# First layer's loop: rows sent ahead of the lists on GpSimd, the token copy moved up, the noise indices' copy moved down, the gate's last remainder moved up

## The chip, the cores and the metric

The kernel runs on one core of one Trainium2 chip. The metric is the device time of one execution in microseconds. All times below are microseconds unless marked ns.

## What is computed

The reference is three stages, one after another, in float32:

- **Attention without a softmax over the keys.** q is softmaxed over its 64 head dimensions, k over its 576 positions; per batch and head (8 by 8) the output is q_s @ (k_sᵀ @ v). The result is 4608 tokens of 512 numbers.
- **Layer one, a mixture of 8 experts with one choice.** `logits = x @ w_gate`, the expert with the largest logit gets the token: `h = relu(x @ w1[e])` with 1024 columns, `y = h @ w2[e]`, times the softmax weight of that expert.
- **Layer two, a mixture of 8 experts with two choices and noise.** `noisy = x @ w_gate + log1p(exp(x @ w_noise)) * noise`; the two largest experts of each token are computed and added with their softmax weights.

## The kernel before

The attention writes one row per token to a table in HBM (`xg`). Tokens are sorted into lists by expert (`lists`, one row of four words per token and choice: token, weight, row of the noise, padding). Both expert layers then go through the lists in blocks of 128 tokens. Every float32 matmul with the weights is done as three fp32r products: high part of x times high part of W, low part of x times high part of W, high part of x times low part of W. So a block costs 96 matmuls of 128x128 by 512 columns: 12 each for the two halves of the first product (`b.m0`, `b.m1`, in PSUM as `pk` and `pkv`), 24 for the second (`b.y0`, `b.y1`, in `pq`); the hidden layer of one block and the output of the block before it run in one turn of the loop, so one turn has 48 of them.

**The loop in question** is `step1` (line 569), the body of `moe1`'s loop over the blocks of layer one; it runs 38 times. Each engine runs its own instructions in the order in which `step1` writes them, and semaphores hold it where it needs another's result. One turn does, beside the 48 matmuls:

- **The gate of layer two** for the 128 tokens that the turn before produced (`x2r`, written by ScalarE in `b.result()`, line 545). TensorE transposes them (`gate_pe1`), ScalarE and VectorE split them into three bf16 parts: `part16` is ScalarE's cast, `rest16` (line 309) VectorE's remainder. `gate_parts` makes the first part and the first remainder, `gate_parts2` the second part and the last remainder (both take the same two lines, 304 and 309). `gate_products` (line 326) has TensorE multiply the three parts with the gate's weights: 12 small matmuls, the last four of which read the last remainder. The sum, three activations and two chains of small VectorE operations (`gate_chain1`, `gate_chain2`) give each token's two experts; `gate_rank` (line 388) has TensorE rank the tokens of each expert, from `g_os` (line 374), and `gate_places` (line 403) gives each token its places in the lists (`g_di`).
- **GpSimd's four kinds of transfer.** `send_list` adds to a table (`dump`, line 408) and writes the 128 tokens with two indirect transfers into the lists of layer two (line 411). `send_rows` (line 421) writes the tokens' 128 rows back to `xg`, at the token numbers in `tk`. `gather` (line 271) fetches the 128 rows of a later block from `xg` into `xr`; it waits until the rows sent before it have landed. `gather_noise` (line 277) fetches the noise of the next block into `nz`, at the indices in `ni`.
- **The copies `gate_meta`**: `gate_row` (line 346, marks padding), `ni` (line 562) and `tk` (line 563), all from `meta`, which holds the list rows of four blocks in flight: iB is the block whose output is made, iA the one behind it. `next_meta` (lines 439 and 440) shifts all four on by one.
- **Weights.** Each turn prepares a part of the next expert's weights in two halves: a 512 KB load into `raws[0]` or `raws[1]` (line 151, on SyncE's queue), a high half cast by ScalarE (`prep_hi`, lines 157 to 159) and a low half by VectorE (`prep_lo`, lines 164 and 165, the second of which is the copy called `tick`).
- **SyncE's queue**, in this order: zeros for 128 rows of the output (line 549), two weight loads (line 151), the next list row block into `iN` (`load_list`, line 266, which waits until the lists sent have landed), and four transfers of the hidden layer (`spread`, line 530).
- **The hidden layer's turn**: ScalarE's relu (`relu32`, line 521), VectorE's transpose in blocks of 32 (`turn32`, line 525), `spread` to `hT`, then the high and low parts (`hi32`, line 536, `lo32`, line 541) in the next turn.

The tile framework puts the waits: an instruction that overwrites a tile waits until the transfers that read it are done. So `ni` (line 562) waits for the noise gather of the turn before, and the copy into `tl` (line 369, in `gate_chain2`) waits for the two list transfers of its turn.

Of the kernel before, what the change touches and what calls it, by code (L numbers as in the profile page):

```python
# [73 lines left out]
def reg(eng, expr, lo, hi):  # L74

    return eng.snap(eng.to_reg(expr), min_val=lo, max_val=hi)
# [71 lines left out]
def load_part(nc, z, raw, i, c0=0, n=SL):  # L148

    a = z.wall[i] if isinstance(i, int) else z.wall[ds(i, 1)].rearrange("o p x -> (o p) x")  # L150
    return nc.sync.dma_start(raw, a[:, c0:c0 + n])


def prep_hi(nc, z, off, h):

    raw = z.raws[h]
    nc.scalar.activation(z.touch[h], raw[:, 0:1], AF.Identity, bias=z.tick[h], scale=1.0)
    no_mm(z, nc.scalar.copy(cols(z, off + h * HL, HL), raw), h)  # L158
    nc.scalar.copy(z.touch[h], raw[:, 0:1])  # L159


def prep_lo(nc, z, off, h):
    raw = z.raws[h]
    no_mm(z, nc.vector.tensor_sub(cols(z, off + 8192 + h * HL, HL), raw, f32(cols(z, off + h * HL, HL))), h)  # L164
    nc.vector.tensor_copy(z.tick[h], raw[:, 0:1])
# [89 lines left out]
def transposes(nc, z, out, src):  # L255
    for c in range(4):
        nc.tensor.transpose(out[:, c * 128:(c + 1) * 128], src[:, c * 128:(c + 1) * 128], z.ident)  # L257


def col(z, x, c):  # L260
    return z.meta[:, c, z.cols[id(x)]:z.cols[id(x)] + 1] if id(x) in z.cols else x[:, c:c + 1]


def load_list(nc, z, to, row):

    nc.sync.dma_start(to, z.lists[row:row + 128, :] if isinstance(row, int) else z.lists[ds(row, 128), :])


def gather(nc, z, of, n=None):

    return nc.gpsimd.indirect_dma_start(  # L271
        out=z.xr, out_offset=None, in_=z.xg[0:n, :] if n else z.xg,
        in_offset=bass.IndirectOffsetOnAxis(ap=col(z, of, 2 if n else 0), axis=0))


def gather_noise(nc, z, of):
    nc.gpsimd.indirect_dma_start(
        out=z.nz, out_offset=None, in_=z.noise,
        in_offset=bass.IndirectOffsetOnAxis(ap=of, axis=0))
# [22 lines left out]
def part16(z, i, x):  # L302

    return z.tc.nc.scalar.copy(z.x3[i], x)


def rest16(z, i, x):
    out = z.x2T if i == 0 else z.x3[2]
    return z.tc.nc.vector.tensor_tensor(out, x, z.x3[i], op=OP.subtract)
# [13 lines left out]
def gate_products(nc, z):  # L323
    for i in range(3):
        for c in range(4):
            nc.tensor.matmul(z.pL[:, 0:48], lhsT=z.x3[i][:, c * 128:(c + 1) * 128],
                             rhs=z.w3[:, c].rearrange("p i n -> p (i n)"),
                             start=i == 0 and c == 0, stop=i == 2 and c == 3)


def gate_sum(nc, z):
    nc.vector.tensor_reduce(z.gt["lg"], z.pL[:, 0:48].rearrange("p (i n) -> p n i", i=3), axis=AX.X, op=OP.add)


def gate_act(nc, z):
    a, t = nc.scalar, z.gt

    a.activation(t["ab"], t["lg"][:, 8:16], AF.Abs)
    a.activation(t["e"], t["ab"], AF.Exp, scale=-1.0)
    a.activation(t["ln"], t["e"], AF.Ln, bias=z.ones[:, 0:1], scale=1.0)  # L340


def gate_row(nc, z):

    v, t = nc.vector, z.gt
    v.tensor_scalar(t["nv"], col(z, z.iB, 0), float(N), None, op0=OP.is_ge)


def gate_chain1(nc, z):
    v, t = nc.vector, z.gt  # L350

    v.tensor_scalar(t["u"], t["e"], 1.0, None, op0=OP.add)  # L352
    v.scalar_tensor_tensor(t["c"], t["u"], 1.0, t["e"], op0=OP.subtract, op1=OP.subtract)
    v.reciprocal(t["r"], t["u"])
    v.scalar_tensor_tensor(t["ns"], t["lg"][:, 8:16], 0.0, t["ln"], op0=OP.max, op1=OP.add)
    v.tensor_mul(t["c"], t["c"], t["r"])
    v.tensor_sub(t["ns"], t["ns"], t["c"])
    v.tensor_mul(t["ns"], t["ns"], z.nz)
    v.tensor_add(t["ny"], t["ns"], t["lg"][:, 0:8])
# [26 lines left out]
def gate_rank(nc, z):  # L386
    for i, x in enumerate((z.after, z.ones16)):
        nc.tensor.matmul(z.pL[:, 48 + i * E:48 + (i + 1) * E], lhsT=x, rhs=z.gt["os"], start=True, stop=True)


def gate_ends(nc, z):
    v = nc.vector
    v.tensor_tensor(z.gt["rg"], z.pL[:, 48:48 + E], z.ends2, op=OP.add)
    v.tensor_tensor(z.ends2, z.pL[:, 48 + E:48 + 2 * E], z.ends2, op=OP.add)
# [11 lines left out]
def send_list(nc, z):  # L406
    t = z.gt
    nc.gpsimd.tensor_tensor(z.dump, z.dump, z.c256, op=OP.add)
    for k in range(2):
        nc.gpsimd.tensor_tensor(z.spacer, t["di"], t["di"], op=OP.add)  # L410
        i = nc.gpsimd.indirect_dma_start(  # L411
            out=z.lists, out_offset=bass.IndirectOffsetOnAxis(ap=t["di"][:, k:k + 1], axis=0),
            in_=z.tl[:, k, :], in_offset=None)
        z.tc.add_to_no_dep_group("list2", i.ins)
        z.tc.declare_no_dep(i.ins, group="list2", across_iterations=True,
                            reason="each token and choice has its own row")


def send_rows(nc, z, of=None):

    i = nc.gpsimd.indirect_dma_start(
        out=z.xg, out_offset=bass.IndirectOffsetOnAxis(ap=col(z, z.iB, 0) if of is None else of, axis=0),
        in_=z.x2r[:, 0:512], in_offset=None)
    z.sent = i
    for o in z.before_rows:
        z.tc.declare_no_dep(i.ins, o.ins, reason="it reads the rows of tokens that are in no block before it")
    z.tc.add_to_no_dep_group("xg2", i.ins)
    z.tc.declare_no_dep(i.ins, group="xg2", across_iterations=True, reason="each token has its own row")
# [8 lines left out]
def next_meta(nc, z, n=3):  # L437

    nc.vector.tensor_copy(f32(z.meta[:, :, 0:n]), f32(z.meta[:, :, 1:n + 1]))
    nc.vector.tensor_copy(f32(z.meta[:, :, n]), f32(z.iN))  # L440


def turn_x(nc, z):
    transposes(nc, z, z.pX, z.xr)


def make_xhi(nc, z):
    nc.scalar.copy(flat(z.xhi), z.pX)
# [7 lines left out]
def make_xlo(nc, z):  # L456
    nc.vector.tensor_sub(flat(z.xlo), z.pX, f32(flat(z.xhi)))
# [17 lines left out]
def tab_value(eng, tab, row, g, max_val):  # L475
    return eng.value_load(tab[0:1, ds(g + row * 128, 1)], min_val=0, max_val=max_val)
# [71 lines left out]
def zero_rows(nc, z, zr):  # L548
    nc.sync.dma_start(z.out[zr:zr + 128, :] if isinstance(zr, int) else z.out[ds(zr, 128), :], z.yo)


def gate_parts(nc, z):

    gate_pe1(nc, z)
    part16(z, 0, z.pS)
    rest16(z, 0, z.pS)


def gate_meta(nc, z):

    gate_row(nc, z)
    nc.vector.tensor_copy(z.ni, col(z, z.iA, 2))
    nc.vector.tensor_copy(z.tk, col(z, z.iB, 0))


def gate_parts2(nc, z):
    part16(z, 1, z.x2T)
    rest16(z, 1, z.x2T)


def step1(tc, z, g, tab, wm, wy, then):


    nc = tc.nc
    a, v, sp = nc.scalar, nc.vector, nc.sync

    part0 = tab_value(sp, tab, 1, g, 2 * E * K - 1)
    part = tab_value(sp, tab, 1, g + 1, 2 * E * K - 1)
    row = tab_value(sp, tab, 2, g + 3, 2 * E * CAP - 128)
    oa = tab_value(a, tab, 0, g, SLOT + (K - 1) * SL)  # L580
    ov = tab_value(v, tab, 0, g, SLOT + (K - 1) * SL)
    b = Block(z, (wm, wy), True)
    zero_rows(nc, z, reg(sp, smin(g + 2, NT - 1) * 128, 0, N - 128))
    load_part(nc, z, z.raws[0], part0, 0, HL)
    send_list(nc, z)
    b.m0.go(4)
    gate_parts(nc, z)
    prep_hi(nc, z, oa, 1)
    prep_lo(nc, z, ov, 1)
    load_part(nc, z, z.raws[1], part, HL, HL)  # L590
    gate_meta(nc, z)
    send_rows(nc, z, z.tk)
    next_meta(nc, z)
    load_list(nc, z, z.iN, row)
    b.m0.go(8)
    then()
    b.relu32(0)
    b.turn32(0)
    gate_parts2(nc, z)
    for i in range(2):  # L600
        b.hi32(i)
        b.lo32(i)
    b.m1.go(12)
    b.relu32(1)
    b.turn32(1)
    turn_x(nc, z)
    gate_products(nc, z)
    make_xhi(nc, z)
    gather(nc, z, z.iP)
    gate_sum(nc, z)  # L610
    gate_act(nc, z)
    prep_hi(nc, z, oa, 0)
    b.spread()
    make_xlo(nc, z)
    gate_chain1(nc, z)
    gather_noise(nc, z, z.ni)
    gate_chain2(nc, z, z.tk)
    b.y0.go(12)
    b.y1.go(10)
    gate_rank(nc, z)  # L620
    b.y1.go(2)
    gate_ends(nc, z)
    gate_weights(nc, z)
    gate_places(nc, z)
    prep_lo(nc, z, ov, 0)
    b.result()
# [1197 lines left out]
```

## Time and profile before

| | |
|---|---|
| median of 3 runs | 1591.85 us (1590.35 to 1595.33) |
| the profiled execution's own time | 1599.28 us |
| its span in the profile | 1596.7 us |
| TensorE busy | 1515.0 us, 95% of the span |
| VectorE, ScalarE, GpSimd busy | 70%, 54%, 36% |
| mean granted TensorE clock | 0.988 of full speed |

A busy share is an average over the attention (to about 185 us), layer one's loop (to about 716 us), a passage between, and layer two. An engine's idle time counts only where it holds up what sets the end. In the views below, the note in square brackets behind a row is the engine's idle time just ahead of it and what ended it.

### The profile page before, as it was taken

The page shows a single profiled execution, that of the slowest core. Times are in us where ns is not written, and L with a number is a line of the kernel's source. Part 1 is how long each engine was busy: PE and PEld are TensorE (multiplying, and loading weights), DVE is VectorE, ACT ScalarE, POOL GpSimd, SP SyncE. Part 2 cuts the span into 40 slices and gives each one's busy share as a digit, 9 for nine tenths or more (in the row PEclk, how much of TensorE's full clock was granted, in tenths as well). Part 3 has the DMA queues.
Part 4 walks back from the last instruction along what each step waited for, and adds up shares of the span by engine and source line. Part 5 has one row for each costly group of instructions (what it writes and reads, how often), then busy time and mean ns, then how long its engine had stood idle before and what let it go on. Part 6 is the DMA issues. An engine that isn't in the chain of part 4 may idle for free.

```text
span 1596.7 us, 44299 instructions
## 1 busy us (share of the span) xinstructions
PE 1515.0 (95%) x7996; PEld 1216.0 (76%) x7996; DVE 1122.4 (70%) x3052; ACT 867.1 (54%) x1914; POOL 571.4 (36%) x625
## 2 busy tenths in 40 slices
PE   8997899999998999978999999999999999999997
PEld 6876677777776777756788888888887878878885
DVE  6888688877887878875666666666666666666665
ACT  7775355555555555544455555545555555555554
POOL 4576455455444455434222222222222212222221
PEclk9999999999999999999999999999999999999998
DMA  9897666665566556652777787777878777778877
GB/s 323 271 300 207 182 179 177 178 178 143 174 178 174 162 178 156 178 161 59 199 211 213 214 215 218 206 210 210 218 212 206 218 204 212 217 202 219 214 211 184
DMA packets 217312, 318.29 MB, mean 199 GB/s; under 512 B 45312, under 2 KB 143104, under 8 KB 217280
## 3 DMA queue, kind: packets, MB, share of 16 engines
q1 hardware_dynamic: 188624, 255.87, 52.7%
q0 software_dynamic: 28656, 62.03, 18.9%
q8 instruction: 15, 0.25, 0.1%
q14 instruction: 17, 0.14, 0.0%
HBM read 186.85 MB, written 52.31 MB: 150 GB/s over the span
## 4 chain that ended last, share of the span: by engine, by line
PE 51%; DMA 1%; DVE 1%; issue 1%; ACT 0%; SPq 0%; POOLq 0%; ACTq 0%; DVEq 0%
PE pq L243 25%; PE pk L243 13%; PE pkv L243 13%; DMA hT<-h 0%; DMA out<-yo,meta 0%; DMA li<-lists 0%; SPq L530 0%; DMA xr<-xg,li 0%; POOLq L1820 0%; DVE g_u L352 0%; DVE h L525 0%; DVE hlo L513 0%; ACT hhi L536 0%; DVE W L164 0%; PE px L257 0%
## 5 line engine op out<-in xcount | busy, mean ns | idle before, releaser
L243 PE MATMUL pq<-W,hhi 128*128 (+1 forms) x1856 | 495.6, 397 | 6.3 <-ACT W L208 5.0
L243 PEld LDWEIGHTS pq<-W,hhi 128*128 128x128 f32 x1856 | 344.6, 189 | 77.9 <-ACT W L208 5.4
L271 POOL DMA_INDIRECT xr<-xg,meta x114 | 114.7, 1006 | 660.6 <-DVE h L525 436.3
L164 DVE TENSOR_TENSOR W<-raw,W 128x1024 f32 x226 | 277.3, 1227 | 58.5 <-ACT touch L159 39.8
L243 PE MATMUL pk<-W,xhi 128*128 (+1 forms) x936 | 261.8, 401 | 6.3 <-ACT x L1001 2.0
L243 PE MATMUL pkv<-W,xhi 128*128 (+1 forms) x936 | 257.7, 397 | 0.0
L536 ACT CAST hhi<-hT 128x512 fp32r<-128x512 f32 x224 | 127.9, 620 | 233.0 <-PE pkv L243 116.9
L243 PE MATMUL pq<-W,hlo 128*128 (+1 forms) x928 | 252.8, 394 | 0.0
L158 ACT CAST W<-raw 128x1024 f32 x226 | 234.1, 1036 | 0.0
L243 PEld LDWEIGHTS pk<-W,xhi 128*128 128x128 f32 x936 | 174.4, 189 | 59.4 <-issue 19.9
L243 PEld LDWEIGHTS pkv<-W,xhi 128*128 128x128 f32 x936 | 176.9, 189 | 42.9 <-issue 0.4
L243 PEld LDWEIGHTS pq<-W,hlo 128*128 128x128 f32 x928 | 174.3, 189 | 40.1 <-DVE hlo L541 3.0
L541 DVE TENSOR_TENSOR hlo<-hT,hhi 128x512 fp32r<-128x512 f32 x224 | 144.6, 687 | 75.9 <-ACT hhi L536 75.9
L432 POOL DMA_INDIRECT out<-yo,meta x76 | 120.5, 1585 | 179.0 <-issue 176.4
L525 DVE STREAM_TRANSPOSE h<-h 128x512 f32<-128x512 f32 x226 | 160.1, 708 | 9.4 <-ACT h L521 5.3
L462 DVE STREAM_TRANSPOSE raw<-xr 128x512 f32<-128x512 f32 x74 | 81.7, 1104 | 115.7 <-DMA hT<-h 58.6
L243 PE MATMUL pk<-W,xlo 128*128 (+1 forms) x468 | 132.5, 405 | 0.0
L243 PE MATMUL pkv<-W,xlo 128*128 (+1 forms) x468 | 130.2, 399 | 0.0
L471 ACT CAST xhi<-raw 128x512 fp32r<-128x512 f32 x74 | 46.0, 622 | 146.0 <-DMA raw<-raw 118.2
L411 POOL DMA_INDIRECT lists<-tl,g_di x80 | 99.6, 1245 | 16.6 <-issue 13.4
L243 PEld LDWEIGHTS pkv<-W,xlo 128*128 128x128 f32 x468 | 88.0, 188 | 21.4
L243 PEld LDWEIGHTS pk<-W,xlo 128*128 128x128 f32 x468 | 85.8, 190 | 18.5 <-issue 0.2
(315 smaller groups left out, 1823.5 us busy)
## 6 DMA issues: line engine op xcount, KB each, us to landing
raw<-in_wall SPq DMA_DIRECT2D x237, 512.0 KB
hT<-h SPq DMA_DIRECT2D x452, 128.0 KB
raw<-raw SPq DMA_DIRECT2D x296, 64.0 KB
out<-yo SPq DMA_DIRECT2D x41, 256.0 KB
A<-in_q SPq DMA_DIRECT2D x36, 256.0 KB
xg<-xrow SPq DMA_DIRECT2D x36, 256.0 KB
A<-in_v SPq DMA_DIRECT2D x8, 1024.0 KB
A<-in_kT SPq DMA_DIRECT2D x6, 1152.0 KB
```

The source lines that it names most:

```text
L158: no_mm(z, nc.scalar.copy(cols(z, off + h * HL, HL), raw), h)
L164: no_mm(z, nc.vector.tensor_sub(cols(z, off + 8192 + h * HL, HL), raw, f32(cols(z, off + h * HL, HL))), h)
L243: i = z.tc.nc.tensor.matmul(self.out, lhsT=a, rhs=cols(z, self.wo + c, 512), start=self.start and self.n == 0, stop=self.stop and self.n = ...
L271: return nc.gpsimd.indirect_dma_start(out=z.xr, out_offset=None, in_=z.xg[0:n, :] if n else z.xg, in_offset=bass.IndirectOffsetOnAxis(ap=c ...
L411: i = nc.gpsimd.indirect_dma_start(out=z.lists, out_offset=bass.IndirectOffsetOnAxis(ap=t["di"][:, k:k + 1], axis=0), in_=z.tl[:, k, :], i ...
L432: nc.gpsimd.indirect_dma_start(out=z.out, out_offset=bass.IndirectOffsetOnAxis(ap=col(z, z.iB, 0), axis=0), in_=z.yo, in_offset=None, comp ...
L462: nc.vector.transpose(out=z.x32.rearrange("p (c k t) -> p c k t", c=4, k=4), in_=z.xr.rearrange("p (k j c) -> p c k j", k=4, c=4))
L471: nc.scalar.copy(hi, x)
L525: self.nc.vector.transpose(out=to, in_=self.z.h[:, i * 512:(i + 1) * 512].rearrange("p (c x) -> p c x", c=4))
L536: self.nc.scalar.copy(self.z.hhi[i].rearrange("p k (q t) -> p k q t", q=4), self.part32(i))
L541: self.nc.vector.tensor_sub(x, self.part32(i), f32(y))
```

## The change

In `step1`, `gate_meta` and `send_rows` go from behind the second weight load to the front, ahead of `send_list`. `gate_meta` loses the copy into `ni`; it is done late in the turn, after the second `turn32`, from iB, since `next_meta` has by then moved iA's rows there. `gate_parts2` goes from behind the first `turn32` to where `gate_meta` was, directly behind `prep_hi` and `prep_lo` of the second half. Nothing is added or dropped: each turn has the same instructions.

```diff
@@ gate_meta
     gate_row(nc, z)
-    nc.vector.tensor_copy(z.ni, col(z, z.iA, 2))
     nc.vector.tensor_copy(z.tk, col(z, z.iB, 0))
@@ step1
     load_part(nc, z, z.raws[0], part0, 0, HL)
+    gate_meta(nc, z)
+    send_rows(nc, z, z.tk)
     send_list(nc, z)
     b.m0.go(4)
     gate_parts(nc, z)
     prep_hi(nc, z, oa, 1)
     prep_lo(nc, z, ov, 1)
     load_part(nc, z, z.raws[1], part, HL, HL)
-    gate_meta(nc, z)
-    send_rows(nc, z, z.tk)
+    gate_parts2(nc, z)
     next_meta(nc, z)
     load_list(nc, z, z.iN, row)
     b.m0.go(8)
     then()
     b.relu32(0)
     b.turn32(0)
-    gate_parts2(nc, z)
     for i in range(2):
         b.hi32(i)
         b.lo32(i)
     b.m1.go(12)
     b.relu32(1)
     b.turn32(1)
+    nc.vector.tensor_copy(z.ni, col(z, z.iB, 2))
     turn_x(nc, z)
     gate_products(nc, z)
```

## Rows read from the trace of the kernel before

**Rows 1.** Stretches: length, busy PE, PEld, DVE, ACT, POOL; granted clock, transfers' share, GB/s.
```profile
190.00:716.00 526.00, 493.06 (x2644) 385.95 (x2642) 422.09 (x1671) 296.88 (x719) 258.50 (x302) 0.99 0.60 171
...
512.50:518.00 5.50, 5.41 (x19) 4.38 (x20) 4.77 (x23) 2.23 (x8) 1.93 (x2) 0.64 0.46 103
...
452.40:465.80 13.40, 12.96 (x71) 10.20 (x70) 11.07 (x45) 7.84 (x19) 6.59 (x8) 1.00 0.63 143
```

**Rows 2.** Line 421, the rows sent: duration, first and last start, time to landing.
```profile
L421 POOL DMA_INDIRECT xg<-x,tk x38: 960/960/1118, 193.9 to 703.1; - x38
...
DMA to landing us min/median/max: 2.7/5.2/7.5
```

**Rows 3.** Groups by line, 190 to 716 us: busy, mean ns, idle before and releasers.
```profile
L326 PE MATMUL px<-w,x 128*128 128x48 bf16 x456 | 24.2, 184 | 22.7 <-issue 10.1 <-DVE x L309 9.7 <-DVE h L525 3.0
...
L369 DVE COPY tl<-tk 128x2 int32<-128x2 int32 x38 | 5.9, 155 | 1.7 <-DMA lists<-tl,g_di 1.7
...
L562 DVE COPY ni<-meta 128x1 int32<-128x1 int32 x38 | 5.5, 145 | 8.9 <-DMA nz<-in_noise,ni 8.9
```

**Rows 4.** Timeline of TensorE in one turn: start, duration, line, operation, idle before.
```profile
453.57 0.27 PE L326 MATMUL px<-w,x 128*128 128x48 bf16 x4 [0.32 <-issue]
```

**Rows 5.** Timeline of VectorE in the same turn.
```profile
448.52 0.15 DVE L165 COPY tick<-raw 128x1 f32<-128x1 f32 x1
...
450.04 1.24 DVE L164 TENSOR_TENSOR W<-raw,W 128x1024 f32 x1 [0.60 <-ACT touch L159]
...
451.27 0.14 DVE L346 TENSOR_SCALAR g_nv<-meta 128x1 f32<-128x1 int32 x1
...
451.65 0.17 DVE L439 COPY meta<-meta 128x12 f32<-128x12 f32 x1
...
452.87 0.65 DVE L309 TENSOR_TENSOR x<-x,x 128x512 bf16<-128x512 f32 x1
...
457.84 0.15 DVE L369 COPY tl<-tk 128x2 int32<-128x2 int32 x1
...
458.37 0.17 DVE L374 TENSOR_TENSOR g_os<-g_oh 128x8 bf16<-128x8 f32 x1
```

**Rows 6.** Timeline of ScalarE in the same turn: the second part's cast.
```profile
450.33 0.61 ACT L304 CAST x<-x 128x512 bf16<-128x512 f32 x1
```

**Rows 7.** Timeline of GpSimd in this turn and the two behind it.
```profile
447.61 1.05 POOL L408 TENSOR_TENSOR dump<-dump,c 128x2 f32<-128x2 f32 x1 [0.76 <-DVE g_di L403]
...
450.35 1.80 POOL L411 DMA_INDIRECT lists<-tl,g_di  x1 [0.16 <-issue]
452.45 0.96 POOL L421 DMA_INDIRECT xg<-x,tk  x1 [0.30 <-DVE meta L440]
459.50 0.97 POOL L271 DMA_INDIRECT xr<-xg,meta  x1 [6.09 <-DVE ends L394]
...
464.86 1.00 POOL L411 DMA_INDIRECT lists<-tl,g_di  x1 [0.15 <-issue]
...
477.31 2.05 POOL L411 DMA_INDIRECT lists<-tl,g_di  x1 [0.16 <-issue]
```

**Rows 8.** Timeline of SyncE's queue, from this turn into the next but one.
```profile
458.22 2.51 SPq L530 DMA_DIRECT2D hT<-h  x4
...
464.69 1.44 SPq L151 DMA_DIRECT2D raw<-in_wall  x2
471.88 0.33 SPq L266 DMA_DIRECT2D iN<-lists  x1
472.70 2.53 SPq L530 DMA_DIRECT2D hT<-h  x4
...
480.31 1.04 SPq L151 DMA_DIRECT2D raw<-in_wall  x2
481.68 0.33 SPq L266 DMA_DIRECT2D iN<-lists  x1
```

**Rows 9.** Waits of SyncE's queue in the loop: total, times, longest.
```profile
SPq L266 <- DMA lists<-tl,g_di: 94.9, 21, 7.1
```

## Prediction

> **What bounds the kernel now.** I read the page first, for TensorE's high share, then busy time by stretch, then the loop's groups by line, and last the timelines of one turn, engine by engine. By stretch, layer one's loop has TensorE busy for only 493.06 of 526.00 us, 33 us short [rows 1]. All that the change touches lies in that loop. Its 38 turns send their rows first at 193.9 and last at 703.1 us [rows 2], so the mean turn takes 509.2/37 = 13.76 us. One common turn, of 13.40 us, holds 12.96 us of TensorE work [rows 1]. So 12.96 is about the least that a turn can take with these matmuls, and 37 x (13.76 - 12.96) = 30 us is the most that a reordering here can bring.
>
> Where are they? The groups by line give most of TensorE's idle time in the loop to one line: 22.7 us stand ahead of the gate's small products (line 326) [rows 3]. The timeline shows how: TensorE idles 0.32 us ahead of the last four products at 453.57, and the next 24 big matmuls come behind them [rows 4]. Those four need the gate's last remainder, which VectorE makes from 452.87 to 453.52 [rows 5]. ScalarE's part for it has been ready since 450.94 [rows 6]: VectorE could have begun when the weights' remainder was done, at 451.28, but first did `gate_row`, the copies, `next_meta` and a transpose [rows 5]. Beyond this small wait there are rare long ones: the copy into `ni` idled VectorE for 8.9 us in all, held by the noise gather of the turn before [rows 3]. That gather is late because GpSimd's fetch of rows, ahead of it, waits until the sent rows have landed: sent at 452.45, fetched at 459.50 [rows 7]; landing took up to 7.5 us [rows 2]. TensorE pays twice: in 512.5 to 518 us, behind the longest of these waits, the granted clock was 0.64, a mix of the levels 1.2 and 2.4 GHz, with TensorE busy for 5.41 of the 5.50 us [rows 1].
>
> **The change, part by part.**
>
> *The last remainder moves up.* It starts at about 451.3 in place of 452.87 and ends near 452.0, well ahead of the products that read it, which could have run at 453.25 [rows 4, 5]. ScalarE does its cast (0.61 us) ahead of the relu in place of behind it [rows 6], so the first transpose's input comes 0.6 us later; the remainder's own 0.65 us on VectorE [rows 5] cover that. Value: all 22.7 us [rows 3], and of the slow stretch 5.50 x (1 - 0.64) = 2.0 us [rows 1]; 24.7 us. Bounds: 24.7 at the most, at the least the small wait alone, 38 x 0.32 = 12.2.
>
> *What is late next.* Behind the products come 22 big matmuls, then the ranking, which needs `g_os`, ready at 458.54 [rows 5]. VectorE works with hardly a gap from 450.04 up to there, so `g_os` comes earlier only by what leaves this stretch: `gate_row` and two copies took 451.27 to 451.65, 0.38 us [rows 5], and `ni` comes back with 0.145 us [rows 3] or less. That is 0.24 to 0.32 us earlier, where TensorE comes 0.32 earlier. So 0 to 0.08 us a turn stays; I take 0.05, near the middle: 38 x 0.05 = 2 us back (0 to 3).
>
> *`gate_row` and `tk` move to the front.* VectorE has `tick` done at 448.67, then the first remainder (0.65 us by the last one's row), then 0.60 us of idling up to 450.04 [rows 5]. The two copies fit into idle time around that remainder: no cost. Without that cover it would be 2 x 0.145 us a turn, 11 us.
>
> *Rows first.* `tk` is ready near 448.9, and with the 0.30 us that a sending shows behind a copy [rows 7] the rows go at 449.2 in place of 452.45, 3.3 us sooner. With 2.7 to 7.5 us [rows 2] they land between 452 and 457. The fetch of rows then waits at most for that or for its buffer to be read, which by the order of `step1` is before 453.57, and no longer stands at the turn's end. The noise gather goes sooner too, behind its index copy near 455 and the reading of `nz`, and VectorE no longer waits for it. Its 8.9 us are not counted again: TensorE's share of them is in the 22.7.
>
> *The price is on the lists.* The two list transfers now stand behind the rows: 449.2 + 0.96, then `dump` (1.05 us [rows 7], since it falls beside a weights' remainder), then two issues of 1.00 to 2.05 us [rows 7] with 0.4 between. The second is done at 453.6 to 455.7, where it was done at 452.15 [rows 7]: 1.5 to 3.5 us later. Who waits for them? VectorE's copy into `tl` at 457.84 [rows 5], with `g_os` queued behind it, and SyncE's list load, with `spread`, the zeros and both weight loads queued behind it. SyncE waits already: 94.9 us in 21 cases [rows 9], free so far because `spread` has time; VectorE waits for 1.7 us in all [rows 3]. When the weights went out at 464.69 and the second list at 464.86, SyncE got on only at 471.88, 7.2 us behind the weights; when that list had gone out by 479.36, ahead of weights at 480.31, the list load went at 481.68, without a wait [rows 7, 8]. In return the rows' 256 KB no longer come with the lists. What it costs no row shows: between nothing and rival 2's circle closed in every turn, 37 x (14.48 - 13.05) = 53 us. I take 1 us, near the lower end, because the rows now find transfer engines that are busy for only 0.60 of the loop [rows 1].
>
> *`ni` late.* It must only precede the noise gather. No cost beyond its 0.145 us above.
>
> **Sum**, against the profiled execution's own 1599.3 us (its span of 1596.7 and 2.6 around it): 1599.3 - 22.7 - 2.0 + 2 + 1 = 1577.6; I forecast 1577. The median of the runs, 1591.85, lies 7.4 us below that execution. I put this down to the rare long waits, which can differ from run to run and which the change takes away. So the sum needs no correction, but the gain against the median is 15 us, not 22.
>
> **Rivals.**
>
> 1. *The time goes to the copy into `tl`.* The lists come 0.3 to 0.4 us after VectorE wants them, in most turns. For it: they are issued 1.5 us later or more, and the copy wants them 0.3 us sooner. Against it: the second issue already varies by a microsecond [rows 7], and this wait shows three times at most now. Price: 37 x 0.35 = 13 us back on the sum, 1590: no difference.
>
> 2. *SyncE's queue sets the pace (slower).* Its own circle: lists in, `spread` 0.82 us behind the list load (471.88 to 472.70), weights 6.47 behind `spread` (458.22 to 464.69), lists in 7.19 behind the weights [rows 8]. That is 14.48 us, longer than a turn; kept closed in every turn it is 37 x (14.48 - 13.76) = 27 us over today. Today it opens whenever the second list goes out ahead of the weights, as before 480.31 [rows 7, 8]. With the lists later it may stay closed. The point that decides: whether the lists need more than 13.0 - 7.3 = 5.7 us behind the weights. Closed in three turns of four: 37 x (0.75 x 14.48 + 0.25 x 13.05 - 13.76) = 13 us above the profiled execution, 1613.
>
> 3. *The lists are not held up by the weights at all.* Then turns run at TensorE's floor with 0.05 us of waiting: 37 x (13.76 - 13.01) = 28 us, 1571. Against it stands 471.88, 7.0 us behind the second list's issue at 464.86 [rows 7, 8]. The Trainium skill's page "DMA: Bandwidth & Descriptors" (Queues, rings and completion order) says that each transfer engine takes turns between the queues it has work for, a packet at a time; by that the lists' few packets would pass between the weights' and come early, as in this rival. The row speaks against it, so it gets well under half of the forecast's chance.
>
> **How the numbers follow.** Forecast 0.50, rival 1 0.18, rival 2 0.14, rival 3 0.18. About 0.3%, 4.8 us, is what a measurement of this kernel can tell from no change: faster is below 1587.1, slower above 1596.6. Forecast and rival 3 are faster, 0.68; rival 1 is the same, 0.18; rival 2 is slower, 0.14. The range starts at 1566, just under the floor of 1599.3 - 30 = 1569, since runs of before differ by 5 us among themselves. It ends at 1597: the forecast with the least of its main term (12.2 for 24.7) is 1590, rival 1 lies within, rival 2 outside.
>
> **What would show it.** Right: no idle time ahead of the last four products, line 326's 22.7 us down to under 3; no wait at `ni`; rows sent some 3 us sooner; the fetch of rows in the middle of the turn; turns of 13.0 to 13.2 us. Rival 1: idle time at line 369 far above 1.7 us. Rival 2: nearly all list loads waiting, turns over 14 us, ScalarE waiting for weights or `hT`. The forecast is wrong if TensorE waits over 0.2 us a turn at the ranking, or if the mean turn stays above 13.4 us.

## The result, and the profile after

The changed kernel takes 1604.81 us (median of 15 runs, 1596.01 to 1613.80) where the kernel before takes 1591.85 (15 runs, 1585.66 to 1597.36): ratio 1.0084, 95% interval [1.0063, 1.0106]. It is slower, by 13 us, and outside the forecast's range of 1566 to 1597. The profiled execution took 1603.47 us with a span of 1601.1.

The loop first. Line 421, duration, first and last start:

```profile
L421 POOL DMA_INDIRECT xg<-x,tk x38: 977/991/1554, 187.3 to 706.2; - x38
```

(706.2 - 187.3)/37 = 14.02 us a turn, where it was 13.76 [rows 2]; the forecast wanted 13.0 to 13.2. The groups by line, 190 to 716 us (busy, mean ns, idle before and its releasers):

```profile
L410 POOL TENSOR_TENSOR spacer<-g_di 128x2 int32<-128x2 int32 x75 | 46.0, 613 | 1.1
...
L157 ACT ACTIVATE touch<-raw,tick 128x1 f32<-128x1 f32 x75 | 22.1, 295 | 14.6 <-DMA raw<-in_wall 14.3
...
L326 PE MATMUL px<-w,x 128*128 128x48 bf16 x456 | 17.5, 183 | 0.0
...
L369 DVE COPY tl<-tk 128x2 int32<-128x2 int32 x38 | 6.6, 175 | 33.1 <-DMA lists<-tl,g_di 33.0
...
L388 PE MATMUL px<-g_os,after 128*128 128x8 bf16 x37 | 6.2, 168 | 26.4 <-DVE g_os L374 26.4
...
L605 DVE COPY ni<-meta 128x1 int32<-128x1 int32 x38 | 4.1, 109 | 0.0
```

Both waits that the change aims at are gone: 22.7 us ahead of line 326 are 0.0, and 8.9 us at `ni` are 0.0 [rows 3]. But the copy into `tl`, 1.7 us before [rows 3], now idles VectorE for 33.1, and through `g_os` TensorE idles for 26.4 at the ranking (line 388). SyncE's queue waits for the same transfers; this is its row in the list of waits (total, times, longest):

```profile
SPq L266 <- DMA lists<-tl,g_di: 206.6, 36, 6.7
```

It was 94.9 in 21 turns [rows 9]; now it is nearly every turn. The list leaves out waits for which it finds no releaser, or names another one, so the queue's own timeline says more: before, the list load came under 3 us behind the start of the weight loads in 9 of 38 turns, and 4.9 us or more behind it in the other 29; now it comes 6.0 us or more behind it in all 38. SyncE's queue in two turns of the changed kernel (start, duration, line):

```profile
448.22 2.53 SPq L530 DMA_DIRECT2D hT<-h  x4
453.76 0.38 SPq L549 DMA_DIRECT2D out<-yo  x1
454.47 1.02 SPq L151 DMA_DIRECT2D raw<-in_wall  x2
462.14 0.33 SPq L266 DMA_DIRECT2D iN<-lists  x1
462.96 2.51 SPq L530 DMA_DIRECT2D hT<-h  x4
468.36 0.38 SPq L549 DMA_DIRECT2D out<-yo  x1
469.06 1.02 SPq L151 DMA_DIRECT2D raw<-in_wall  x2
476.60 0.33 SPq L266 DMA_DIRECT2D iN<-lists  x1
477.42 2.53 SPq L530 DMA_DIRECT2D hT<-h  x4
```

From `spread` to the weights 6.25 and 6.10 us, from the weights to the list load 7.67 and 7.54, from there to the next `spread` 0.82 and 0.82: 14.74 and 14.46 us. That is the circle of rival 2, closed turn after turn. These two turns are longer than most: over the loop the three legs are 6.22, 7.04 and 0.82 us on average. That they add up to the turn shows nothing, as they do so in any loop; what speaks for the circle is that nothing else holds the queue: besides the list load's, its list of waits has 1.5 us in all. GpSimd in the first of these turns:

```profile
452.37 0.99 POOL L421 DMA_INDIRECT xg<-x,tk  x1 [4.95 <-DVE x L309]
453.39 0.80 POOL L408 TENSOR_TENSOR dump<-dump,c 128x2 f32<-128x2 f32 x1
454.15 0.70 POOL L410 TENSOR_TENSOR spacer<-g_di 128x2 int32<-128x2 int32 x1
455.00 1.00 POOL L411 DMA_INDIRECT lists<-tl,g_di  x1 [0.16 <-issue]
456.04 0.57 POOL L410 TENSOR_TENSOR spacer<-g_di 128x2 int32<-128x2 int32 x1
456.77 1.24 POOL L411 DMA_INDIRECT lists<-tl,g_di  x1 [0.16 <-DVE hlo L541]
```

And VectorE in this turn:

```profile
449.61 0.22 DVE L403 SCALAR_TENSOR_TENSOR g_di<-dump,g_nv,g_S 128x2 int32<-128x2 f32 x1
...
451.36 0.14 DVE L562 COPY tk<-meta 128x1 int32<-128x1 int32 x1
...
454.12 0.68 DVE L309 TENSOR_TENSOR x<-x,x 128x512 bf16<-128x512 f32 x1
...
455.91 1.25 DVE L541 TENSOR_TENSOR hlo<-hT,hhi 128x512 fp32r<-128x512 f32 x2
...
462.03 0.17 DVE L369 COPY tl<-tk 128x2 int32<-128x2 int32 x1 [1.61 <-DMA lists<-tl,g_di]
```

For comparison the places `g_di`, and `tk`, in the turn of before that the prediction read (VectorE's timeline):

```profile
447.21 0.22 DVE L403 SCALAR_TENSOR_TENSOR g_di<-dump,g_nv,g_S 128x2 int32<-128x2 f32 x1
...
451.39 0.14 DVE L563 COPY tk<-meta 128x1 int32<-128x1 int32 x1
```

Counted from the end of `g_di`, 447.43 before and 449.83 after, the second list's issue ends at 452.15 - 447.43 = 4.72 us before [rows 7] and at 458.01 - 449.83 = 8.18 us after, 3.46 us later. The weights go out at 454.47, 3.5 us ahead of that; the lists that the list load waits for are in 462.14 - 458.01 = 4.13 us behind their issue.

TensorE can pay for such a wait twice, as it did in the slow stretch of before [rows 1]. It stood 1.52 us ahead of the ranking at 462.77; the stretch behind it (length, busy PE, PEld, DVE, ACT, POOL, granted clock, transfers' share, GB/s):

```profile
464.00:470.00 6.00, 6.00 (x22) 4.93 (x22) 4.54 (x14) 3.80 (x9) 2.80 (x3) 0.72 0.62 172
```

A granted clock of 0.72 is a mix of the two levels, 1.2 and 2.4 GHz, with TensorE busy all the time. Most waits cost only once: of TensorE's 20 waits of over 0.7 us in the loop, three were followed by a lower clock (0.81 in 280 to 289 us, 0.83 in 351 to 361 and in 463 to 473), and the longest, 1.88 us at 533.46, was not (1.00 in 531 to 541).

### The profile page after: what moved, and what is told of

It reads as the page before. It is cut to its first block, busy times and chain, and to the rows that moved or that the text cites. A ratio compares the mean times of both kernels' runs of the same rounds, so it can differ in the third digit from the quotient of the medians.

```text
span 1601.1 us, 44185 instructions
## 1 busy us (share of the span) xinstructions
PE 1517.0 (95%) x7996; PEld 1225.2 (77%) x7996; DVE 1129.1 (71%) x3052; ACT 868.6 (54%) x1914; POOL 581.6 (36%) x625
## 4 chain that ended last, share of the span: by engine, by line
PE 52%; DVE 1%; DMA 1%; issue 0%; ACT 0%; SPq 0%; POOLq 0%; ACTq 0%; DVEq 0%
PE pq L243 26%; PE pk L243 13%; PE pkv L243 13%; DMA li<-lists 0%; DMA hT<-h 0%; DMA xr<-xg,li 0%; DVE g_u L352 0%; SPq L530 0%; POOLq L1820 0%; DVE hlo L513 0%; ACT hhi L536 0%; DVE W L164 0%; PE px L257 0%; ACT W L208 0%; ACT W L158 0%
## 5 line engine op out<-in xcount | busy, mean ns | idle before, releaser
L432 POOL DMA_INDIRECT out<-yo,meta x76 | 120.5, 1585 | 173.4 <-issue 169.4
L421 POOL DMA_INDIRECT xg<-x,tk x38 | 38.2, 1006 | 193.9 <-DVE x L309 152.5
```

Source lines behind the costliest of these rows:

```text
L421: i = nc.gpsimd.indirect_dma_start(out=z.xg, out_offset=bass.IndirectOffsetOnAxis(ap=col(z, z.iB, 0) if of is None else of, axis=0), in_=z ...
L432: nc.gpsimd.indirect_dma_start(out=z.out, out_offset=bass.IndirectOffsetOnAxis(ap=col(z, z.iB, 0), axis=0), in_=z.yo, in_offset=None, comp ...
```

## The experiments

Four theories were set against each other. **S**: SyncE's queue is a closed circle (late lists hold the list load, that holds `spread` and the next weights, and these hold the next lists), and this is the whole loss. **V**: the moved remainder costs something itself, on VectorE or ScalarE. **G**: the time follows GpSimd's order; each microsecond by which the second list is issued sooner is worth time of its own. **T**: only VectorE's wait at `tl` costs, and SyncE's is free. The circle counts as closed in a turn in which the lists come late behind the weights and hold up the queue, and as open or cut where they don't. All ratios are against the kernel before, run on the same chip.

**1. The remainder alone**: the kernel before with only this moved; it stands behind the copies and the sending of the rows here, which stay where they were.

```diff
     gate_meta(nc, z)
     send_rows(nc, z, z.tk)
+    gate_parts2(nc, z)
     next_meta(nc, z)
...
     b.turn32(0)
-    gate_parts2(nc, z)
```

> The kernel before with one part of the change: the last remainder (second call of the gate's parts) directly behind the first weights' remainder; rows sent, tk and ni stay where they were. Theory S (the late lists and SyncE's queue set the turn: the lists go out behind the weights, hold up the list load, the hidden layer's spread and so the next weights, which hold the next lists): the second list goes out as early as before, so the circle opens as before; the small products' 22.7 us fall under 3, VectorE's wait at the copy into tl stays under 8 us, mean turn 13.0 to 13.4 us, 1570 to 1588 us. Rival V (the moved remainder itself costs, by the order on ScalarE and VectorE): 1600 us or more, with TensorE waiting for the hidden layer or the ranking though the lists are early.

Measured: 1584.99 us, ratio 0.9934 [0.9912, 0.9956]. The rows go at 190.5 first and 688.5 last, 13.46 us a turn. Faster by about 10 us, so V falls: the moved remainder by itself gains. The groups by line show TensorE's wait nearly gone, and VectorE's at `ni` still there:

```profile
L326 PE MATMUL px<-w,x 128*128 128x48 bf16 x447 | 18.0, 183 | 3.1 <-DVE x L309 2.7 <-DVE h L525 0.4
...
L562 DVE COPY ni<-meta 128x1 int32<-128x1 int32 x37 | 5.4, 145 | 7.6 <-DMA nz<-in_noise,ni 7.3 <-issue 0.2
```

Line 326 loses 22.7 - 3.1 = 19.6 us of waiting [rows 3], but the loop gets only 509.2 - 498.0 = 11.2 us shorter. Of the difference, 8.6 - 3.0 = 5.6 us stand ahead of the next turn's first big matmuls, into `pk`, where the trace names no releaser. Their row in the kernel before, and in this run:

```profile
L243 PE MATMUL pk<-W,xhi 128*128 x296 | 83.8, 405 | 3.0 <-issue 0.9
```

```profile
L243 PE MATMUL pk<-W,xhi 128*128 x296 | 83.8, 405 | 8.6 <-issue 8.3 <-ACT g_ed L379 0.3
```

**2. The rows and copies alone**: the changed kernel with the remainder back where it was.

```diff
     load_part(nc, z, z.raws[1], part, HL, HL)
-    gate_parts2(nc, z)
     next_meta(nc, z)
...
     b.turn32(0)
+    gate_parts2(nc, z)
```

> The changed kernel with the last remainder put back behind the first transpose: only rows first, tk first and ni late remain. Theory S: the lists are as late as in the changed kernel, list load waits near 200 us in all, copy into tl waits 15 us or more, mean turn near 14.0 us, 1598 to 1610 us. Rival V: no loss without the moved remainder, 1585 to 1594 us.

Measured: 1595.62 us, ratio 1.0011 [0.9989, 1.0033], 13.86 us a turn, between V's 1585 to 1594 and S's 1598 to 1610, and so in neither. By itself this half brings nothing, though TensorE's wait at line 326 is 0.0 in it too. The groups by line:

```profile
L410 POOL TENSOR_TENSOR spacer<-g_di 128x2 int32<-128x2 int32 x72 | 23.6, 327 | 1.0
...
L326 PE MATMUL px<-w,x 128*128 128x48 bf16 x444 | 20.0, 184 | 0.0
...
L369 DVE COPY tl<-tk 128x2 int32<-128x2 int32 x37 | 7.1, 193 | 24.4 <-DMA lists<-tl,g_di 20.1 <-issue 4.2
```

The wait at `tl` comes with the rows, not with the remainder. S also expected the list load to wait near 200 us in all. The list of waits has 65.3 us in 12 turns; by the queue's timeline the list load comes 5.9 us or more behind the start of the weights in all 38 turns, so the circle is closed here too. Yet the two halves do not add up: one gains 10 us, the other nothing, and together they lose 13. Line 326's wait is 0.0 here already, so in the changed kernel the moved remainder has no such wait left to remove; and the circle is longer there, 7.04 us on average from the weights to the list load against 6.69 here. The first row is a reason for that: GpSimd's `spacer`, two of them ahead of the second list, takes 327 ns here and 613 in the changed kernel, where the moved remainder (454.12 to 454.80) lies beside it. That is 2 x 0.29 = 0.6 us more delay of the lists. That this delay is what lengthens the circle was argued from these rows, not run by itself.

**3. Lists ahead of the rows**: the changed kernel with the two swapped on GpSimd.

```diff
     gate_meta(nc, z)
-    send_rows(nc, z, z.tk)
     send_list(nc, z)
+    send_rows(nc, z, z.tk)
```

> The changed kernel with the two list transfers ahead of the rows again on GpSimd (tk stays at the front, the remainder moved up, ni late). Theory S: the second list goes out near 6 us behind the end of the output's matmuls in place of 9, ahead of the weights in some turns; tl wait under 8 us, 1570 to 1588 us. Rival V: no better than the changed kernel, 1600 us or more.

Measured: 1575.20 us, ratio 0.9877 [0.9837, 0.9918], 13.10 us a turn; the wait at `tl` is 0.8 us in all. The loop is 37 x (14.02 - 13.10) = 34 us shorter than the changed kernel's. Of the whole change, putting the rows ahead of the lists is the one part that loses; without it the time comes out near the forecast's 1577. S and G both say so; what tells them apart is the next run.

**4. The list load behind `spread`**: the changed kernel, rows first, with SyncE's circle cut. The lists are issued just as late.

```diff
     next_meta(nc, z)
-    load_list(nc, z, z.iN, row)
     b.m0.go(8)
...
     b.spread()
+    load_list(nc, z, z.iN, row)
     make_xlo(nc, z)
```

> The changed kernel with the list load behind the hidden layer's four transfers on SyncE's queue, so that late lists no longer hold up spread and the next weights; GpSimd's order is untouched. Theory S: the circle is cut there; weights go out some 3 us sooner in the turn, the lists are in before VectorE wants them or within 0.3 us, tl wait under 10 us in all, 1570 to 1588 us. Rival G (GpSimd's order alone: the lists are in some 4 us behind the second issue whatever SyncE does): tl wait stays near 33 us, 1598 to 1608 us.

Measured: 1566.66 us (1563.10 to 1570.41), ratio 0.9816 [0.9775, 0.9856]. GpSimd's timeline, the rows and the second list:

```profile
450.75 0.99 POOL L421 DMA_INDIRECT xg<-x,tk  x1 [4.13 <-DVE x L309]
...
455.14 1.25 POOL L411 DMA_INDIRECT lists<-tl,g_di  x1 [0.15 <-issue]
```

The second list's issue ends 456.39 - 450.75 = 5.64 us behind the start of the rows, as in the changed kernel (458.01 - 452.37 = 5.64). Nothing on GpSimd has become faster, and the loss is gone, so G falls as its cause. SyncE's timeline of the same turn:

```profile
450.39 2.71 SPq L151 DMA_DIRECT2D raw<-in_wall  x2
456.31 2.53 SPq L530 DMA_DIRECT2D hT<-h  x4
459.29 0.71 SPq L266 DMA_DIRECT2D iN<-lists  x1
```

The weights go out 0.36 us ahead of the rows, where in the changed kernel they went 2.10 us behind them, which is the lead they have on the lists. The lists are then in time for everybody, as the groups by line and the waits of SyncE show:

```profile
L369 DVE COPY tl<-tk 128x2 int32<-128x2 int32 x38 | 5.9, 156 | 1.2 <-DMA lists<-tl,g_di 1.2
```

```profile
SPq L266 <- DMA lists<-tl,g_di: 1.2, 2, 0.8
```

The loop by its stretch, from the first to the last sending of rows, in this kernel

```profile
189.20:672.20 483.00, 473.57 (x2595) 375.63 (x2594) 412.64 (x1628) 290.44 (x704) 265.13 (x297) 1.00 0.63 182
```

and in the changed kernel

```profile
187.30:706.20 518.90, 484.14 (x2594) 383.91 (x2593) 414.34 (x1628) 292.00 (x702) 261.78 (x296) 0.99 0.65 169
```

splits the price of the circle: 518.90 - 483.00 = 35.9 us for 37 turns, of which TensorE's idle time is (518.90 - 484.14) - (483.00 - 473.57) = 25.3, and 484.14 - 473.57 = 10.6 are the same matmuls taking longer. About half of that goes with the lower granted clock in the three stretches named above: 9 x 0.19 + 10 x 0.17 + 10 x 0.17 = 5.1 us. The rest is not explained.

**5. The token copy sooner**: `gate_meta` at the end of the turn before, ahead of the last weights' remainder (and once ahead of the loop).

```diff
     load_part(nc, z, z.raws[0], part0, 0, HL)
-    gate_meta(nc, z)
     send_rows(nc, z, z.tk)
...
     gate_places(nc, z)
+    gate_meta(nc, z)
     prep_lo(nc, z, ov, 0)
```

> The changed kernel with gate_row and tk at the very end of the turn before, ahead of the weights' remainder there (and once before the loop), so that the rows wait only for the output itself. Theory S: rows and both lists go out about 1.3 to 2 us sooner than in the changed kernel (second list done near 7 to 7.8 us behind the end of the output's matmuls in place of 9.1), but still behind the weights at 5.5, so the circle stays closed in most turns: tl wait above 15 us, 1588 to 1604 us. Rival G (each microsecond of the second issue counts by itself): mean turn shorter by the same 1.3 to 2 us, to the floor near 13.0, 1565 to 1575 us.

Measured: 1572.86 us, ratio 0.9887 [0.9835, 0.9939], 13.22 us a turn. The time is what G expected, though the turn is 0.80 us shorter and not 1.3 to 2, and it is a miss for S by its numbers: S had taken it that the circle stays closed in most turns. SyncE's queue in two turns of this run shows why it doesn't:

```profile
442.65 1.02 SPq L151 DMA_DIRECT2D raw<-in_wall  x2
445.32 0.33 SPq L266 DMA_DIRECT2D iN<-lists  x1
...
454.09 2.45 SPq L151 DMA_DIRECT2D raw<-in_wall  x2
461.12 0.33 SPq L266 DMA_DIRECT2D iN<-lists  x1
```

In the first turn the list load follows the weights after 2.67 us, in the second after 7.03. In the first the second list's issue had ended at 442.52, just ahead of the weights; in the second it ended at 459.23, behind them. So it is over the loop: in 7 of the 38 turns the list load follows the start of the weights by under 3 us, and in each of them the second list's issue had ended 0.1 us or more ahead of the weights; in the other 31 it follows by 4.0 us or more. On average this leg is 5.4 us, where it is 7.0 in the changed kernel. This run alone does not tell whether the time falls with GpSimd's issue as such or with this leg; the fourth and the ninth run speak for the leg.

**6. A sixteenth of the weights**: the changed kernel, each weight load 64 columns in place of 1024, with the same order and the same number of transfers.

```diff
-    load_part(nc, z, z.raws[0], part0, 0, HL)
+    load_part(nc, z, z.raws[0][:, 0:64], part0, 0, 64)
...
-    load_part(nc, z, z.raws[1], part, HL, HL)
+    load_part(nc, z, z.raws[1][:, 0:64], part, HL, 64)
```

> The changed kernel with both weight loads of the turn cut to 64 of 1024 columns (the other columns keep older data, so the outputs of layer one's later experts are wrong; all instructions stay). Theory S: with nothing to stand behind, the lists are in within some 3 us of the second issue, tl wait under 3 us, list load waits under 60 us in all, mean turn 12.9 to 13.1 us, one time of 1558 to 1572 us. Rival G: lists come as late as before behind the second issue (some 3.5 to 4 us), tl wait stays above 20 us, 1595 us or more.

One time, 1574.72 us. Layer two sorts other values here and has one block more, so only the loop is compared: rows from 187.5 to 667.9, 12.98 us a turn. Around one turn, SyncE's queue

```profile
448.25 1.02 SPq L151 DMA_DIRECT2D raw<-in_wall  x2
454.12 0.11 SPq L266 DMA_DIRECT2D iN<-lists  x1
```

and GpSimd's second list

```profile
451.32 1.24 POOL L411 DMA_INDIRECT lists<-tl,g_di  x1 [0.16 <-DVE hlo L541]
```

The second list's issue ends at 452.56, 3.29 us behind that of the weights (449.27), and the list load goes 1.56 us later. Of the two turns of the changed kernel shown above, the second has nearly the same distance:

```profile
471.84 1.25 POOL L411 DMA_INDIRECT lists<-tl,g_di  x1 [0.16 <-issue]
```

Its second list's issue ends at 473.09, 3.01 us behind that of the weights (470.08), and the list load goes 3.51 us later. Over the loop it goes 1.3 to 1.8 us behind the second list here (1.56 on average), and 1.5 to 4.6 in the changed kernel (3.40). So it is the bytes of the weights that hold the lists, not their place behind the rows. The list load still stands 4.2 us or more behind the end of the weights' issue in every turn here, and the turn is 12.98 all the same: such a wait costs nothing by itself. The Trainium skill's page "DMA: Bandwidth & Descriptors" (Queues, rings and completion order) has each transfer engine take turns between queues, a packet at a time; by that the lists' few packets would lose little to weights that went out earlier on another queue. The two turns differ in that by 3.51 - 1.56 = 1.95 us, and the measurement decides. How the packets are ordered inside was not tried.

**7. The copy into `tl` late**: the changed kernel, this copy behind the ends' sum, so that `g_os` no longer stands behind it.

```diff
-    v.tensor_copy(z.tl[:, :, 0], (col(z, z.iB, 0) if of is None else of).to_broadcast([128, 2]))
+    if of is None:
+        v.tensor_copy(z.tl[:, :, 0], col(z, z.iB, 0).to_broadcast([128, 2]))
...
     gate_ends(nc, z)
+    nc.vector.tensor_copy(z.tl[:, :, 0], z.tk.to_broadcast([128, 2]))
```

> The changed kernel with the copy into tl behind the ranking's two sums, so that VectorE's wait for the lists no longer holds up g_os; list load and spread stay as they are. Theory S with the circle on SyncE as what binds: the list load still waits near 200 us in all, mean turn stays above 13.7 us, now with waits elsewhere (VectorE at tl behind the ranking, ScalarE for hT or weights), 1592 to 1606 us. Rival T (only VectorE's wait at tl binds, the circle has slack): TensorE's wait at the ranking goes and the mean turn falls to 13.0 to 13.2 us, 1565 to 1578 us.

Measured: 1594.22 us, ratio 1.0022 [0.9994, 1.0050], 13.84 us a turn, 0.18 less than in the changed kernel. The groups by line:

```profile
L157 ACT ACTIVATE touch<-raw,tick 128x1 f32<-128x1 f32 x74 | 21.9, 296 | 84.0 <-DMA raw<-in_wall 81.2 <-issue 2.8
...
L624 DVE COPY tl<-tk 128x2 int32<-128x2 int32 x37 | 6.4, 174 | 36.0 <-DMA lists<-tl,g_di 35.8 <-issue 0.2
```

The ranking no longer waits, and yet the turn stays long: ScalarE now idles 84.0 us for weights, against 14.6. T falls as the cause of the whole loss: that the wait at `tl` held up the ranking is worth 37 x 0.18 = 7 us of the loop. For the rest it was where the circle showed on TensorE, not what made the turn long.

**8. The same cut in the kernel before**: its list load moved behind `spread`, as in the fourth run, and nothing else.

> The kernel before with the list load behind the hidden layer's four transfers and nothing of the change. Theory S: the long waits that came from late transfers get fewer, but the small wait of 0.3 us ahead of the last four products stays in every turn (line 326 near 12 us or more): mean turn 13.3 to 13.5 us, 1576 to 1588 us. If SyncE's order alone were worth what the changed kernel with it brought (mean turn 12.96 us), 1563 to 1572 us.

Measured: 1584.61 us, ratio 0.9973 [0.9946, 1.0001], 13.44 us a turn. So the circle cost the kernel before about 5 us, and by the interval 9 at most. TensorE's wait at line 326 stays, but falls to 14.3:

```profile
L326 PE MATMUL px<-w,x 128*128 128x48 bf16 x456 | 24.1, 184 | 14.3 <-issue 10.1 <-DVE h L525 2.4 <-DVE x L309 1.9
```

So 22.7 - 14.3 = 8.4 us of what the forecast gave to the remainder goes with SyncE's order, without the remainder being moved: the 9.7 us that waited for line 309 are 1.9 here. The wait at `ni` goes with it, from 8.9 us [rows 3] to 0.3, though the rows and the noise indices stay where they were. So, by one profile of each, the rare long waits of before came with SyncE's order too.

**9. Both cuts**: the changed kernel with the edits of the fourth and the fifth run.

> The changed kernel with the list load behind the spread on SyncE and with the token copy at the end of the turn before. S (SyncE's circle is the whole loss): the circle is already cut by the first of the two edits alone, so the second adds nothing: 12.95 to 13.05 us a turn as with that edit alone, 1562 to 1571 us. G (every us that the second issue ends sooner is worth time of its own): the second issue ends some 2 us sooner than with the list load's move alone, and the kernel gains more than 3 us beyond it: under 1563 us.

Measured: 1563.70 us (1562.76 to 1568.59), ratio 0.9827 [0.9781, 0.9873], (667.1 - 186.5)/37 = 12.99 us a turn. It is as S expected: with the circle cut, lists that are issued sooner are worth nothing that these intervals can tell from the fourth run (0.9816 [0.9775, 0.9856]). The fourth and the ninth run's kernels are faster than the kernel before as well: by 1594.58 - 1566.66 = 27.9 and 1592.97 - 1563.70 = 29.3 us in their comparisons.

**10. The circle cut, and the remainder up, rows left behind the lists**: the first and the eighth run's edits on the kernel before.

> The kernel before with the gate's last remainder moved up and the list load behind the spread, rows and indices left where they were. It shows what sending the rows first is worth once SyncE's circle is open. S alone (nothing besides the circle and the remainder's place matters): 13.0 to 13.1 us a turn, 1564 to 1574 us. If the early rows and the late noise indices are worth time of their own: 13.15 to 13.4 us a turn, 1573 to 1584 us, with idle time at the noise tile's users.

Measured: 1574.58 us, ratio 0.9889 [0.9845, 0.9933], (676.6 - 188.8)/37 = 13.18 us a turn, with 2.5 us of waits at `ni` left. By the turns this is what the second of the two expectations said: 37 x (13.18 - 13.05) = 4.8 us behind the fourth run. So the early rows and the late noise indices are worth about 5 us of the loop once the circle is open, by one profile of each; the two intervals overlap, so the total times alone do not settle it.

## Why the prediction was wrong

- **The bound of the loop: right.** The floor of 12.96 us a turn is where the ninth run ends (12.99).
- **The last remainder moves up: right in mechanism, too large in size.** The wait went from 22.7 to 0.0, and by itself the edit gained 1594.58 - 1584.99 = 9.6 us (the medians of that comparison) where the term was 24.7; 9.6 lies below even the lower bound of 12.2, which the interval of that ratio (7 to 14 us) just takes in. The eighth run shows a third of the 22.7 going away with the circle, and the first run shows part of it coming back ahead of `pk`.
- **What is late next: right for the ranking where the lists are on time, but not the whole.** 1.6 us stand ahead of line 388 in the fourth run, 0.04 a turn; the step had 0.05. It left out the next turn's first matmuls, whose idle time goes from 3.0 to 8.6 us in the first run; why they idle is open.
- **`tk` at the front: right.** It is done 451.50 - 449.83 = 1.67 us behind `g_di`; the step's 448.9 is 1.47 behind.
- **Rows first: late.** The step put the sending 0.30 us behind `tk`. It comes 452.37 - 451.50 = 0.87 behind. The note of 0.30 was misread: it is idle time behind GpSimd's own last issue, which ended at 452.15 [rows 7], and the copy in `next_meta` that it names is not one that the sending needs. Where GpSimd had been free longer in the kernel before, as ahead of the rows at 300.92, the sending came 0.84 behind `tk`. Once sent, the rows land in 2.7 to 2.9 us, where it took up to 7.5 [rows 2]: they now go ahead of the weights, and the lists behind them. With `dump` at 0.80 and the spacers at 0.70 and 0.57, the second list's issue ends 3.46 us later than before, at the far end of the step's 1.5 to 3.5.
- **The price on the lists: the step that failed.** "I take 1 us, near the lower end, because the rows now find transfer engines that are busy for only 0.60 of the loop [rows 1]." Measured against the kernel whose circle is cut, it is 35.9 us, and 34 against the one with the lists first, of the 53 that the step had as its upper bound. A mean busy share of 0.60 says nothing of the few microseconds in which 1 MB of weights is ahead of the lists (by the sixth run they are in 1.56 us behind their issue with a sixteenth of the weights, and 3.51 with all of them), and the prediction had read that wait already, 7.2 us behind the weights [rows 8].
- **Rival 2: right in mechanism**, at a chance of 0.14. Its deciding point was 5.7 us from the weights to the list load; the turns shown have 7.67 and 7.54, and its circle of 14.48 came out at 14.46 to 14.74. Its mix of three closed turns in four is (0.75 x 14.48 + 0.25 x 13.05) = 14.12 a turn against 14.02 measured, but that closeness is luck: the circle is closed in all turns, and its legs of 6.22 and 7.04 are shorter on average than the 6.47 and 7.19 read before. The time of 1613 was 9.5 us above the profiled execution's 1603.47. Its own rows spoke for it: 7.19 us of before [rows 8] already lay above the deciding point, and the forecast put the lists later still. Since the weights go out only when `spread` does, lists that come late once keep the next weights late, and so the next lists: the turn that opened the circle before, as at 480.31 [rows 8], needs the lists ahead of the weights, and just that the change took away.
- **Rival 1: its place was right** (33.1 us at `tl`), but the seventh run shows the wait to be for the most part a symptom: taken off the ranking's path, it gave back 7 us. **Rival 3** falls with the sixth run.
- **`ni` late: right**, no wait is left at line 605. The eighth run ends that wait too, by SyncE's order alone, with the rows sent where they were.

Put into the forecast's own sum, the measured price gives 1599.3 - 22.7 - 2.0 + 2 + 35.9 = 1612.5, which is 9 us above the 1603.47 of the changed kernel's profiled execution. Without a price the sum is 1576.6, and the fourth run's profiled execution took 1570.41, 6 us less. Part of that can be what the circle had cost the kernel before, about 5 us by the eighth run; no run separates it.

## What to carry to other kernels

Before an issue is put later, follow every queue that waits for it in order, and ask whether what stands behind that wait comes back as the thing that delays the issue; if it does, compare the circle's length, row by row, with the turn. Such a circle shows as a wait in nearly every turn (36 of 38 here by the list of waits), but neither the wait nor the sum of the legs proves it: the sixth run has such a wait in every turn and loses nothing. What proves it is a cut at one place that leaves the rest as it was. And the engine that idles most need not be the one to mend: moving the waiting load behind the work that others need (the fourth run) was worth 36 us of the loop, moving VectorE's wait 7 us. A mean transfer share of 0.6 is no evidence that a small transfer passes quickly.

## What the runs showed of the hardware

- The few words of the two lists, on GpSimd's queue, were in 3.51 us behind their issue with 1 MB of weights issued 3.0 us ahead on SyncE's, and 1.56 us behind it with a sixteenth of those weights issued 3.3 us ahead.
- GpSimd's `spacer`, an operation on 128 x 2 elements, took 263 ns on average in the loop of before, and 613 in the loop of the changed kernel, where the two shown ran beside VectorE's operations with two tensor inputs (454.15 beside line 309, 456.04 beside line 541); in the ninth run, 267. The row of before is this:

```profile
L410 POOL TENSOR_TENSOR spacer<-g_di 128x2 int32<-128x2 int32 x75 | 19.7, 263 | 1.2
```

- With GpSimd free, an indirect transfer started 0.87 us (after) and 0.84 us (before) behind the end of the small copy that holds its indices.
